# Two layers of linear attention and squared-ReLU MLP on one core: idle steps and new costs in the weave of layer 1, and the pair's weight sums in other buffers

## The chip, the cores and the metric

The kernel runs on one core of a Trainium2 chip. The core has five engines that run side by side and wait for each other through semaphores: TensorE (PE in the profile; its weight loads are PEld), VectorE (DVE), ScalarE (ACT), GpSimd (POOL) and SyncE (SP, which here only issues DMAs). The metric is the device time of one execution in microseconds; lower is better.

## The reference

x has 2048 rows of 576 numbers in float32. Four sublayers follow each other, A, B, A, B, with the same weights both times:

```python
def A(x):                     # linear attention, 32 heads of 18
    q, k, v = split_heads(x @ wqkv)
    phi = lambda t: concat(softmax(t @ w_phi), softmax(-(t @ w_phi)))
    kv, z = einsum("bhsf,bhsd->bhfd", phi(k), v), phi(k).sum(over rows)
    return (phi(q) @ kv / (phi(q) @ z + 1e-6)) @ wo
def B(x):                     # 576 -> 4608 -> 576
    h = x @ w1 + b1
    return relu(h)**2 @ w2 + b2
x = x + A(layernorm(x)); x = x + B(layernorm(x))      # layer 0
x = x + A(layernorm(x)); x = x + B(layernorm(x))      # layer 1
```

The sums kv and z run over all rows, so no row's attention output can be made before all rows' keys and values are in.

## The kernel before, in words

The rows are cut into four blocks of 512, a block into four tiles of 128. Nearly every product is made of three: operands are split into a high and a low part (`hi` by an ACT copy into the matmul's format, `lo` by a subtraction on DVE or POOL), and hi·hi, hi·lo and lo·hi are summed in PSUM. The names in the profile leave numbers out: `m_0` is the MLP of block 0, `a_2` the attention of block 2, `m_p` the pair (below).

The work around the change is in layer 1, whose blocks come in the order 1, 0, 3, 2.

**The weave.** `weave(main, other, rate)` (L99) runs two generators into one program. `main` is the MLP of a block (`g_mlp`), whose loop over 36 feature tiles f is cut into 36 steps; `other` is "the back", the attention work of later blocks. After each main step, `rate` is added to what is due, and steps of the back are issued while at least 1 is due; each takes off its cost, the number that it yields (1.0 where it yields nothing). `paced(gen, cost)` (L111) gives all steps of a generator one cost. `held` (L560) lets a step's instructions follow a given instruction of the MLP on its engine. The order of each engine is fixed when the program is built: the framework goes by the order in which instructions are written, and takes a later one first where it expects the earlier one still to wait. On the chip each engine then runs its queue strictly in that order, so an instruction that waits holds up what is queued behind it.

One main step, an MLP iteration: `first(f+1)` loads and splits weights (L697 to L709), `hidden(f)` makes 14 matmuls (L719), `square(f)` applies bias, ReLU and square on ACT (L726 to L728) and the low part on DVE (L729, the `hl` of the profile's `m_0hb`), and `second(f-1)` makes 15 matmuls of the second product (L746, L737). So the result of `square(f)` is wanted one iteration later. The last rows of a block are taken through buffers of tag "x" and written out (L785 to L793).

The back of the first weave of layer 1 (main: block 1, rate 3.6): features of block 0 (`g_features`: four softmax steps of cost 5.5, then per row tile two steps of cost 2.8 that divide by the denominators on DVE and POOL, L584 to L594), queries of block 3 (four steps, 1.0), output of block 0 (`g_out`: one step, ten of transposing and multiplying with kv, L624 and L640, and one, at 1.0 each), features of block 3, and then, for each row tile, the product with wo, the residual and the norm of block 0 (five steps, 3.0).

The back of the second weave (main: block 0, rate 4.3): output of block 3; its norm (`g_norm_first`: four steps with the product with wo at L673, then six that transpose, L818 and L826, and evict, L843 to L847; the result is spilled to memory, L850); queries of block 2 (four steps; they read spilled rows back, L374), features of block 2, output of block 2; its norm (`g_norm_second`, likewise four steps and then six). These six are four `main` tiles and, after the second and the fourth, a `tail`. In `g_norm_second` each is *combined*: from the two halves of the spilled block and of this one, `combine` (L893) makes the operands b22, t1, t2, t3, t4, and each is split; a main tile has six DVE operations there, five ACT copies (L917), two POOL sums (L905, L907) and four POOL low parts (L918). All ten steps of either norm cost 3.0. Then the prelude of the pair (seven steps, 2.0).

**PSUM.** In layer 1's weaves the back's transposes and products take tiles of tag "w", of which there are two; each must be evicted by ACT and DVE before it is used again.

**The pair.** The MLPs of blocks 3 and 2 are done together (`g_pair`), 18 times a pair of feature tiles: the first product of both blocks with two feature tiles is made by seven half-size products (L1007) in place of eight, which need sums of the weight quarters a11, a12, a21, a22. `load_pair` loads the quarters: a11 and a12 in one buffer, a21 and a22 in another, in turn of two pairs. `split_pair` makes the sums on POOL and splits the seven operands (hi L966 on ACT, lo L967 on DVE, a small band L969 on POOL):

```python
s1 = a21 + a22     # ss[0], L972
s2 = s1 - a11      # ss[1], L975
s4 = a12 - s2      # ss[3], L979
s3 = a11 - a21     # ss[2], L982
```

The four sums are in buffers of tag "x" (five buffers), which the rows of `g_mlp`'s end, of `g_out` and the temporaries of `combine` use too. The splits for pair k+1 are written between the products of pair k. In the products, u and v (tag "qk", five buffers) take the eviction of PSUM (L1117, L1118, L1121, L1122), and are written to memory (`hd`, L1125 and L1075) for the second block; `product(k, bx, "a22", ...)` can go on in bank bx only after L1122 has read it. The first pair's first products stand ahead of the last rows of the second weave's MLP.

Of the kernel before, what the change touches and what calls it, by code (L numbers as in the profile page):

```python
# [7 lines left out]
F32 = mybir.dt.float32  # L8
# [5 lines left out]
P = 128  # L14
# [7 lines left out]
def layers_kernel(  # L22
# [18 lines left out]
    nc = tc.nc  # L41
    S, D = x_in.shape[1], x_in.shape[2]
# [17 lines left out]
    HK = HP // P  # L60
# [8 lines left out]
    sb = ctx.enter_context(tc.tile_pool(name="sb", bufs=2))  # L69
# [39 lines left out]
        drain(other)  # L109

    def paced(gen, cost):  # L111
        for _ in gen:
            yield cost

    def lagged(n, produce, consume, by=1):

# [27 lines left out]
    for p, g in ((GW, slice(0, full)), (gw[full], slice(full, NG))):  # L144
        n = g.stop - g.start
# [165 lines left out]
    def moments(x, t, name):  # L311
        stats = sb.tile([P, 2, 6], F32, tag="bns", name=f"{name}s{t}")
        mv = sb.tile([P, 2], F32, tag="bnm", name=f"{name}m{t}")
        rstd = sb.tile([P, 1], F32, tag="rstd", name=f"{name}d{t}")
        for h in range(2):
            nc.vector.bn_stats(stats[:, h, :], x[:, h * HP : (h + 1) * HP])
        nc.vector.bn_aggr(mv, stats.rearrange("p a b -> p (a b)"))
        nc.gpsimd.tensor_scalar(rstd, mv[:, 1:2], EPS, None, op0=ALU.add)
        nc.gpsimd.tensor_tensor(rstd, rstd, mhalf, op=ALU.pow)
        return mv, rstd  # L320
# [472 lines left out]
            nc.sync.dma_start(out[b * TB + t * P : b * TB + (t + 1) * P] if layer else xs[b][t], x)  # L793


    def g_norm_halves(x_of, name, then, main, tail):

        xd = sb.tile([P, NT, 2 * TP], F32, tag="xd", name=f"{name}e", bufs=1)
        xns = []
        for t in range(NT):  # L800
            x = x_of(t)
            mv, rstd = moments(x, t, name)
            xn = sb.tile([P, D], F32, tag="qk", name=f"{name}n{t}", bufs=5)[:, : KC * P]
            x3 = x.rearrange("p (a d) -> p a d", a=2)
            nc.vector.tensor_scalar(xn.rearrange("p (a d) -> p a d", a=2), x3[:, :, : HK * P], mv[:, 0:1], rstd,
                                    op0=ALU.subtract, op1=ALU.mult)
            nc.vector.tensor_scalar(xd[:, t].rearrange("p (a r d) -> p a r d", a=2, r=3),
                                    x3[:, :, HK * P :].unsqueeze(2).to_broadcast([P, 2, 3, TW]),
                                    mv[:, 0:1], rstd, op0=ALU.subtract, op1=ALU.mult)
            then(t, x)  # L810
            xns.append(xn)
            yield
        for t in range(NT):
            pt = wtile(f"{name}p{t}")
            p4 = pt.rearrange("p (a c n) -> p a c n", a=2, n=P)
            for a in range(2):
                for c in range(HK):
                    nc.tensor.transpose(p4[:, a, c], xns[t][:, (a * HK + c) * P : (a * HK + c + 1) * P], ident)  # L818
            main(t, p4)
            yield  # L820
            if t % 2:
                pt = wtile(f"{name}p{NT}{t}")
                p3 = pt[:TP].rearrange("p (a n) -> p a n", a=2)
                for a in range(2):
                    for i in range(2):
                        nc.tensor.transpose(p3[:, a, i * P : (i + 1) * P],  # L826
                                            xd[:, t - 1 + i, a * TP : (a + 1) * TP], ident)
                tail(t // 2, p3)
                yield

    def g_norm_first(x_of, dst, name, then):

        tiles = {}

        def main(t, p4):
            if t == 0:
                tiles.update(xt_tiles(name))
                tiles["t"] = sb.tile([P, 2 * D], F32, tag="E", name=f"{name}t", bufs=4)[:TP, : 2 * TB]
                tiles["t"] = tiles["t"].rearrange("p (a n) -> p a n", a=2)
            rows = slice(t * P, (t + 1) * P)  # L840
            hi, lo = tiles["h"][:, :KC, rows], tiles["l"][:, :, rows]
            p3 = p4.rearrange("p a c n -> p (a c) n")
            nc.scalar.activation(hi, p3, AF.Copy)  # L843
            nc.vector.tensor_sub(lo, p3, hi.bitcast(F32))

        def tail(h, p3):
            nc.scalar.activation(tiles["t"][:, :, h * TB // 2 : (h + 1) * TB // 2], p3, AF.Copy)  # L847

        yield from g_norm_halves(x_of, name, then, main, tail)
        nc.sync.dma_start(pth, tiles["h"][:, :KC].rearrange("p c n -> p (c n)").bitcast(F32))  # L850
        nc.sync.dma_start(ptl, tiles["l"].rearrange("p c n -> p (c n)").bitcast(F32))
        nc.sync.dma_start(ptt, tiles["t"].rearrange("p a n -> p (a n)"))

    def g_norm_second(x_of, dst, name, then):
# [68 lines left out]
                split_tail(ops[k][2][:, cols], src)  # L923

        prepare()
        yield from g_norm_halves(x_of, name, then, main, tail)
        dst.update(ops)

    def g_pair(layer, blocks, x, after, name):
# [16 lines left out]

        def split_pair(k, raw):
            (a11, a12), (a21, a22) = raw
            ss = [sb.tile([P, D], F32, tag="x", name=f"{name}s{j}_{k}", bufs=5)[:, : (HK + 1) * P]
                  .rearrange("p (c n) -> p c n", c=HK + 1) for j in range(4)]  # L950
            width = NC * P
            if k % 2 == 0:
                one = sb.tile([P, NC * HP], F32R, tag="h1", name=f"{name}wa_{k}")
                two = sb.tile([P, NC, P], F32, tag="r1", name=f"{name}wb_{k}").rearrange("p c n -> p (c n)")
                homes = [new_slot(j, f"{name}wv{j}_{k}", F32R) for j in range(NT)] + [one[:, :width], one[:, width : 2 * width], two.bitcast(F32R)]
            else:
                t = xt_tiles(f"{name}wc_{k}")
                flat = [t[p].rearrange("p c n -> p (c n)") for p in "hl"]
                homes = [flat[0][:, j * width : (j + 1) * width] for j in range(4)]
                homes += [flat[1][:, j * width : (j + 1) * width] for j in range(3)]  # L960
            homes = dict(zip(("a11", "a12", "s1", "s2", "s4", "s3", "a22"), homes))

            def split(key, src):
                op = homes[key].rearrange("p (c n) -> p c n", c=NC)
                hi, lo = op[:, : HK + 1], op[:, HK + 1 :]
                nc.scalar.activation(hi, src, AF.Copy)  # L966
                nc.vector.tensor_sub(lo, src[:, :HK], hi[:, :HK].bitcast(F32))  # L967
                band = slice(2 * TW, 3 * TW)
                nc.gpsimd.tensor_sub(hi[band, HK], src[band, HK], hi[band, HK].bitcast(F32))  # L969
                wops[k, key] = (hi, lo)  # L970

            nc.gpsimd.tensor_add(ss[0], a21, a22)  # L972
            split("a11", a11)
            yield
            nc.gpsimd.tensor_sub(ss[1], ss[0], a11)  # L975
            split("a12", a12)
            yield
            split("s1", ss[0])
            nc.gpsimd.tensor_sub(ss[3], a12, ss[1])  # L979
            yield  # L980
            split("s2", ss[1])
            nc.gpsimd.tensor_sub(ss[2], a11, a21)  # L982
            yield
            split("s4", ss[3])
            yield
            split("s3", ss[2])
            yield
            split("a22", a22)
            yield
# [176 lines left out]
    def g_attend(layer, b, x, raws, dst, name, behind=None, norm=None, mid=(None, None), ph=None):  # L1166

        cost = (lambda c: c) if layer else (lambda c: None)
        if ph is None:
            ph = []  # L1170
            if raws is None:
                raws = []
                yield from g_queries(layer, b, x, raws, name)
            yield from g_features(layer, raws, ph, name)
        if mid[0]:
            yield from mid[0]
        yield from g_out(layer, b, ph, dst, name, behind=behind and behind["last"], norm=norm, mid=mid[1],
                         costs=(cost(1.0), cost(3.0)))

    def g_features(layer, raws, ph, name):  # L1180
        cost = (lambda c: c) if layer else (lambda c: None)
        er = []
        yield from paced(held(g_soft(raws, er, name)), cost(5.5))
        yield from paced(held(g_phi(layer, er, ph, name, True)), cost(2.8))
# [68 lines left out]
    x, xprev = xT[b], xT[prev]  # L1253
    for layer in range(2):
# [7 lines left out]
        for i, b in enumerate(order):  # L1262
            n = f"{layer}_{b}"
# [38 lines left out]
            back = g_back()  # L1302

            def then(back=back):
# [1 line left out]
                next(products)  # L1306

            weave(g_mlp(layer, b, ready, rows, f"m{n}", None if i else dense["turned"], then if layer and i == 1 else None),
                  back, (3.6, 4.3)[i] if layer else 1.5 if i else 1.0)
            ready, nxt_raws = nxt, None  # L1310
            if layer == 0:
                prev_rows = (b, rows)
        if layer == 0:
# [3 lines left out]
            x, xprev, vpair = {}, keep["x"], keep["v"]  # L1317
# [29 lines left out]
```

## Time and profile before

| | us |
|---|---|
| median of three runs | 2567.29 |
| lowest, highest run | 2564.45, 2567.36 |
| the profiled execution | 2566.98 |
| its span, first to last instruction | 2565.3 |

In the profile, L719 is line 719 of the kernel. A row of the timeline reads: start in us, duration in us, engine, line, operation, output and inputs, shapes, count, and in brackets the engine's idle time before it with what ended it. A row of a group reads: line, engine, operation, output and inputs, shapes, count, busy us in total, mean ns of one, idle us before and what ended it. A row of the stretches reads: from:to, length, then for PE, PEld, DVE, ACT and POOL the busy us and the number of instructions, the clock granted to TensorE (1.00 is full speed), and the DMA engines' busy share and GB/s.

### The profile page before, as it was taken

The numbers are of one execution on the slowest core, as the hardware profiler recorded it, in microseconds if no ns is written. First come the engines' busy times: TensorE is split into PE (matmuls) and PEld (weight loads), VectorE is DVE, ScalarE is ACT, GpSimd is POOL, SyncE is SP. The second block draws the span as 40 slices with busy tenths as digits, with TensorE's granted clock in tenths as the row PEclk, the third lists the DMA queues.
The fourth block names the chain that finished last, engine by engine and source line by source line (L and its number), as shares of the span: only waits on it lengthen the run. The fifth ranks groups of instructions, "written<-read, shape, count | busy, mean of one in ns | idle before, by whom it ended". The sixth has DMA issues, their size and how long they took to land. (4 is left out here: it accounts for less than half of the span.)

```text
span 2565.3 us, 41355 instructions
## 1 busy us (share of the span) xinstructions
PE 2508.4 (98%) x15282; PEld 2205.9 (86%) x15282; DVE 1540.2 (60%) x2408; ACT 1268.4 (49%) x2177; POOL 804.9 (31%) x869
## 2 busy tenths in 40 slices
PE   8998999999999999999999999999999999999999
PEld 8998888888888888888888988888888877888888
DVE  6778844456655467556434788484658565554444
ACT  4334554545554455545554445554455365666543
POOL 3544311113222132123111423132214256555222
PEclk9999999999999999999999999999999999999999
DMA  8102332354333533243433143233453333333364
GB/s 251 57 23 89 103 115 87 104 187 133 89 97 106 181 127 97 84 128 104 118 98 106 45 132 114 79 98 106 143 175 98 119 111 124 111 104 102 105 205 148
DMA packets 276758, 295.03 MB, mean 115 GB/s; under 512 B 28906, under 2 KB 206826, under 8 KB 274250
## 3 DMA queue, kind: packets, MB, share of 16 engines
q1 hardware_dynamic: 275296, 289.68, 36.7%
q8 instruction: 119, 1.95, 0.3%
q10 hardware_dynamic: 1258, 2.70, 0.3%
q14 instruction: 85, 0.70, 0.1%
HBM read 249.39 MB, written 42.89 MB: 114 GB/s over the span
## 5 line engine op out<-in xcount | busy, mean ns | idle before, releaser
L746 PE MATMUL m_0acc<-m_0s,m_0hb 128*128 128x448 f32 x864 | 200.2, 366 | 2.2 <-DVE m_0hb L729 2.2
L746 PE MATMUL m_1acc<-m_1s,m_1hb 128*128 128x448 f32 x864 | 199.2, 366 | 0.5 <-DVE m_1hb L729 0.5
L719 PE MATMUL m_0ph<-a_0nh,m_0h 128*128 128x512 f32 (+1 forms) x760 | 196.1, 386 | 3.4 <-ACT m_0hr L726 3.0
L746 PEld LDWEIGHTS m_0acc<-m_0s,m_0hb 128*128 128x128 f32 x864 | 161.6, 188 | 24.7 <-DVE m_0hb L729 3.9
L746 PEld LDWEIGHTS m_1acc<-m_1s,m_1hb 128*128 128x128 f32 x864 | 161.9, 188 | 21.4 <-DVE m_1hb L729 0.9
L719 PEld LDWEIGHTS m_0ph<-a_0nh,m_0h 128*128 128x128 f32 x760 | 136.4, 189 | 29.7 <-ACT m_0hr L726 3.7
L709 POOL TENSOR_TENSOR m_0s<-m_0r,m_0s 128x128 fp32r<-128x128 f32 x72 | 59.5, 826 | 316.0 <-ACT m_0s L705 279.9
L709 POOL TENSOR_TENSOR m_1s<-m_1r,m_1s 128x128 fp32r<-128x128 f32 x72 | 57.3, 795 | 306.4 <-ACT m_1s L705 274.4
L707 DVE TENSOR_TENSOR m_1h<-m_1r,m_1h 128x640 fp32r<-128x640 f32 x72 | 65.6, 912 | 121.6 <-ACT m_1h L704 121.5
L726 ACT ACTIVATE m_0hr<-m_0ph,b1t 128x512 f32<-128x512 f32 x72 | 49.3, 685 | 169.8 <-PE m_0ph L719 169.8
L707 DVE TENSOR_TENSOR m_0h<-m_0r,m_0h 128x640 fp32r<-128x640 f32 x72 | 65.9, 916 | 111.8 <-ACT m_0h L704 109.7
L726 ACT ACTIVATE m_1hr<-m_1ph,b1t 128x512 f32<-128x512 f32 x72 | 49.5, 688 | 152.7 <-PE m_1ph L719 152.7
L996 DVE TENSOR_TENSOR m_ps<-m_pr,m_ps 128x448 fp32r<-128x448 f32 x72 | 51.7, 718 | 97.5 <-ACT m_ps L995 96.6
L997 POOL TENSOR_TENSOR m_ps<-m_pr,m_ps 128x128 fp32r<-128x128 f32 x72 | 59.2, 822 | 133.9 <-ACT m_ps L995 127.9
L746 PE MATMUL m_2acc<-m_2s,m_2hb 128*128 128x448 f32 x432 | 99.7, 366 | 1.3 <-DVE m_2hb L729 1.3
L746 PE MATMUL m_3acc<-m_3s,m_3hb 128*128 128x448 f32 x432 | 99.5, 366 | 1.0 <-DVE m_3hb L729 1.0
L719 PE MATMUL m_1ph<-t1onh,m_1h 128*128 128x512 f32 (+1 forms) x380 | 97.5, 385 | 0.6 <-ACT t1onh L347 0.6
L719 PE MATMUL m_2ph<-a_2nh,m_2h 128*128 128x512 f32 (+1 forms) x380 | 97.2, 384 | 0.2 <-DVE m_2h L707 0.2
L719 PE MATMUL m_3ph<-t0onh,m_3h 128*128 128x512 f32 (+1 forms) x380 | 95.7, 382 | 0.1
L719 PE MATMUL m_1ph<-a_1nh,m_1h 128*128 128x512 f32 (+1 forms) x380 | 95.2, 381 | 0.0
L1036 PE MATMUL m_pacc<-m_ps,m_phb 128*128 128x448 f32 x432 | 93.9, 366 | 0.0
L995 ACT ACTIVATE m_ps<-m_pr 128x576 fp32r<-128x576 f32 x72 | 49.2, 684 | 87.9 <-PE m_pacacc L1026 65.7
(2103 smaller groups left out, 7131.5 us busy)
## 6 DMA issues: line engine op xcount, KB each, us to landing
m_0r<-in_B_w SPq DMA_DIRECT2D x72, 288.0 KB
m_1r<-in_B_w SPq DMA_DIRECT2D x72, 288.0 KB
m_pr<-in_B_w SPq DMA_DIRECT2D x72, 288.0 KB
m_0r<-in_B_w SPq DMA_DIRECT2D x72, 256.0 KB
m_1r<-in_B_w SPq DMA_DIRECT2D x72, 256.0 KB
m_3r<-in_B_w SPq DMA_DIRECT2D x36, 288.0 KB
m_2r<-in_B_w SPq DMA_DIRECT2D x36, 288.0 KB
m_3r<-in_B_w SPq DMA_DIRECT2D x36, 256.0 KB
```

Of the source, the lines that this page charges most:

```text
L707: nc.vector.tensor_sub(l1, r1, h1.bitcast(F32))
L709: nc.gpsimd.tensor_sub(s2[:, D + R : 2 * D], r2[:, R:], s2[:, R:D].bitcast(F32))
L719: nc.tensor.matmul(ph[:, cols], a, m, start=(k == 0), stop=(k == len(ops) - 1))
L726: nc.scalar.activation(hr, ph, AF.Relu, bias=b1t[:, f : f + 1])
L746: nc.tensor.matmul(acc[t][:, :R], a[:, rows], m, start=(f == 0 and k == 0), stop=(f == NF - 1 and k == 2))
L995: nc.scalar.activation(s2[:, :D], r2, AF.Copy)
L996: nc.vector.tensor_sub(s2[:, D : D + R], r2[:, :R], s2[:, :R].bitcast(F32))
L997: nc.gpsimd.tensor_sub(s2[:, D + R : 2 * D], r2[:, R:], s2[:, R:D].bitcast(F32))
L1036: nc.tensor.matmul(accs[b][t][:, :R], a[:, rows], m, start=(g == 0 and k == 0), stop=(g == NF - 1 and k == 2))
```

## The change

Three things are edited. The steps of the back of layer 1 get an idle step of cost 5.0 (a `yield` that issues nothing) ahead of each output, and the rates of its two weaves go from 3.6 and 4.3 to 3.7 and 5.0. In both norms by halves the four steps with the product with wo keep 3.0, while the six transposed tiles cost 1.0 in `g_norm_first` and 5.0 in `g_norm_second`; `paced` passes a generator's own cost on where its own is None. In `split_pair` s1 and s2 move to buffers of tag "qk", s3 is written over a21 and s4 over a12, and the order of the POOL operations changes. The number of compute instructions stays as it is.

```diff
     def paced(gen, cost):
-        for _ in gen:
-            yield cost
+        for own in gen:
+            yield own if cost is None else cost
...
-    def g_norm_halves(x_of, name, then, main, tail):
+    def g_norm_halves(x_of, name, then, main, tail, cost):
...
             then(t, x)
             xns.append(xn)
-            yield
+            yield 3.0
         for t in range(NT):
...
             main(t, p4)
-            yield
+            yield cost
             if t % 2:
...
                 tail(t // 2, p3)
-                yield
+                yield cost
...
     def g_norm_first(x_of, dst, name, then):
...
-        yield from g_norm_halves(x_of, name, then, main, tail)
+        yield from g_norm_halves(x_of, name, then, main, tail, 1.0)
...
     def g_norm_second(x_of, dst, name, then):
...
-        yield from g_norm_halves(x_of, name, then, main, tail)
+        yield from g_norm_halves(x_of, name, then, main, tail, 5.0)
...
         def split_pair(k, raw):
             (a11, a12), (a21, a22) = raw
-            ss = [sb.tile([P, D], F32, tag="x", name=f"{name}s{j}_{k}", bufs=5)[:, : (HK + 1) * P]
-                  .rearrange("p (c n) -> p c n", c=HK + 1) for j in range(4)]
+            ss = [sb.tile([P, D], F32, tag="qk", name=f"{name}s{j}_{k}", bufs=5)[:, : (HK + 1) * P]
+                  .rearrange("p (c n) -> p c n", c=HK + 1) for j in range(2)]
...
             nc.gpsimd.tensor_sub(ss[1], ss[0], a11)
             split("a12", a12)
             yield
+            nc.gpsimd.tensor_sub(a21, a11, a21)
             split("s1", ss[0])
-            nc.gpsimd.tensor_sub(ss[3], a12, ss[1])
-            yield
+            yield
+            nc.gpsimd.tensor_sub(a12, a12, ss[1])
             split("s2", ss[1])
-            nc.gpsimd.tensor_sub(ss[2], a11, a21)
-            yield
-            split("s4", ss[3])
-            yield
-            split("s3", ss[2])
+            yield
+            split("s4", a12)
+            yield
+            split("s3", a21)
             yield
             split("a22", a22)
             yield
...
     def g_attend(layer, b, x, raws, dst, name, behind=None, norm=None, mid=(None, None), ph=None):
...
             yield from g_features(layer, raws, ph, name)
+        if layer:
+            yield 5.0
         if mid[0]:
             yield from mid[0]
         yield from g_out(layer, b, ph, dst, name, behind=behind and behind["last"], norm=norm, mid=mid[1],
-                         costs=(cost(1.0), cost(3.0)))
+                         costs=(cost(1.0), cost(None if norm else 3.0)))
...
             weave(g_mlp(layer, b, ready, rows, f"m{n}", None if i else dense["turned"], then if layer and i == 1 else None),
-                  back, (3.6, 4.3)[i] if layer else 1.5 if i else 1.0)
+                  back, (3.7, 5.0)[i] if layer else 1.5 if i else 1.0)
```

## The prediction

> **What bounds the kernel now.** The page comes first: its head says how full each engine is.
>
> ```profile
> span 2565.3 us, 41355 instructions
> PE 2508.4 (98%) x15282; PEld 2205.9 (86%) x15282; DVE 1540.2 (60%) x2408; ACT 1268.4 (49%) x2177; POOL 804.9 (31%) x869
> ```
>
> PE works 2508.4 of 2565.3 us; the change alters no matmul, so it can win only PE's idle time, 56.9 us, and stretches in which PE is slow. It touches layer 1 alone, so the second view is the busy time by stretch from there on (length, then PE, PEld, DVE, ACT, POOL busy, granted clock, DMA):
>
> ```profile
> 1530.00:1800.00 270.00, 270.00 (x1354) 235.05 (x1353) 176.23 (x264) 139.54 (x223) 70.22 (x69) 0.99 0.35 103
> 1905.00:1975.00 70.00, 70.00 (x363) 61.99 (x362) 51.58 (x67) 38.49 (x61) 21.30 (x17) 1.00 0.28 82
> 1975.00:1993.00 18.00, 15.43 (x71) 12.25 (x70) 16.76 (x25) 7.51 (x12) 7.95 (x6) 1.00 0.46 134
> 1993.00:2066.00 73.00, 73.00 (x400) 63.81 (x399) 38.69 (x71) 31.44 (x55) 18.90 (x25) 1.00 0.35 110
> 2066.00:2097.00 31.00, 25.67 (x114) 20.86 (x113) 24.00 (x45) 20.49 (x47) 22.55 (x29) 0.94 0.29 85
> 2097.00:2127.00 30.00, 30.00 (x138) 25.11 (x137) 19.29 (x34) 17.37 (x33) 15.21 (x21) 1.00 0.49 150
> 2127.00:2138.00 11.00, 7.21 (x25) 5.32 (x24) 8.33 (x13) 6.31 (x12) 9.74 (x14) 0.84 0.33 98
> 2138.00:2440.00 302.00, 302.00 (x1346) 251.72 (x1346) 147.69 (x242) 187.38 (x344) 153.82 (x199) 1.00 0.35 111
> ```
>
> The first weave of layer 1 (1530 to 1800) and the pair's steady part (2138 to 2440) have no idle PE, so there is nothing to win there. Three holes are left, all in or just behind the second weave: 2.6 us at 1975, 5.3 at 2066, 3.8 at 2127. The waits of PE name them (waiter, awaited, us in total, times, longest):
>
> ```profile
> PE m_ppx L1007 <- DVE m_pu L1122: 3.4, 1, 3.4
> ...
> PE m_0ph L719 <- ACT m_0hr L726: 3.0, 2, 2.0
> ...
> PE a_2np L818 <- DVE a_2nl L918: 1.7, 1, 1.7
> ...
> PE a_2pn L640 <- DVE a_2fl L627: 1.2, 1, 1.2
> ...
> PE a_2qp L387 <- DMA a_2uh<-xth: 0.6, 1, 0.6
> ```
>
> In two of the holes the clock falls as well:
>
> ```profile
> 2072.88:2076.29 3.41, 3.13 (x7) 2.48 (x8) 2.90 (x6) 3.04 (x7) 0.64 (x2) 0.51 0.02 5
> 2134.41:2137.82 3.41, 3.12 (x8) 2.48 (x8) 2.48 (x5) 2.23 (x5) 2.70 (x4) 0.51 0.31 92
> ```
>
> Each has about 3.12 us of matmuls at half speed; at full speed they would take 1.56, so each costs 1.56 us beside its wait. The holes with their slow stretches come to 2.6 + 5.3 + 1.6 + 3.8 + 1.6 = 14.9 us, the DMA wait to 0.6. That is the most there is to win.
>
> **The change part by part.** Where each step lands is arithmetic on the code: every main step adds the rate, every step behind is issued while at least 1 is due and takes off its cost. I number the 36 main steps of a weave.
>
> *Combined tiles at 5.0, idle step, rate 5.0 (second weave).* Before, the second norm's transposed tiles come at steps 28 (main 0), 29 (main 1 and tail 0), 30 (main 2), 31 (main 3 and tail 1), the prelude at 32 to 35. Afterwards they have a step each, 24 to 29, and the prelude takes 30 to 32. The hole at 2066 begins behind the step with two. ACT shows why:
>
> ```profile
> 2070.17 0.42 ACT L917 ACTIVATE a_2nt4h<-a_2nu 128x256 fp32r<-128x256 f32 x1 [1.81 <-POOL a_2nu L907]
> ...
> 2072.44 0.67 ACT L726 ACTIVATE m_0hr<-m_0ph,b1t 128x512 f32<-128x512 f32 x1
> ```
>
> ACT stands 1.81 us for POOL's sum, the copies of main 1 and tail 0 follow, and the MLP's relu (L726) is queued behind them; PE waits for that relu, and for PSUM that the same tiles hold (L818). A main tile gives POOL this:
>
> ```profile
> L918 POOL TENSOR_TENSOR a_2nt1l<-a_2nu,a_2nt1h 128x256 fp32r<-128x256 f32 x1 | 0.7, 744 | 1.8 <-ACT a_2nt1h L917 1.8
> ...
> L918 POOL TENSOR_TENSOR a_2nt4l<-a_2nu,a_2nt4h 128x256 fp32r<-128x256 f32 x1 | 0.7, 737 | 0.0
> ```
>
> Six such operations (four of L918, L905, L907) by 0.74 are 4.4 us. The MLP's own POOL work is one operation an iteration, 0.83 us:
>
> ```profile
> L709 POOL TENSOR_TENSOR m_0s<-m_0r,m_0s 128x128 fp32r<-128x128 f32 x72 | 59.5, 826 | 316.0 <-ACT m_0s L705 279.9
> ```
>
> The 5.2 together fit into one MLP iteration, 6.35 us (five take 31.74, below). Main 0 already stands alone, at 2056, in the stretch 1993 to 2066 without idle PE. So I take the hole as closed: -5.3, and -1.6 for the clock.
>
> [...] The trace has the halving right behind the waits; I go by the trace.
>
> *Idle step ahead of the output, and rate 5.0 (hole at 1975).* The output's first transposes wait for the last feature tile from DVE and POOL. Here is what DVE has to do (five MLP iterations; then one feature tile with one iteration; then the MLP's own three operations in that stretch):
>
> ```profile
> 1928.95:1960.69 31.74, 31.74 (x146) 27.22 (x145) 25.74 (x37) 18.63 (x28) 10.34 (x10) 1.00 0.34 99
> 1964.39:1972.61 8.22, 8.22 (x40) 7.08 (x39) 8.08 (x12) 4.97 (x9) 4.47 (x4) 1.00 0.35 104
> ```
>
> ```profile
> L729 DVE TENSOR_TENSOR m_0hb<-m_0hr,m_0hb 128x512 fp32r<-128x512 f32 x6 | 7.5, 1250 | 0.0
> L707 DVE TENSOR_TENSOR m_0h<-m_0r,m_0h 128x640 fp32r<-128x640 f32 x6 | 7.1, 1188 | 0.0
> ...
> L708 DVE TENSOR_TENSOR m_0s<-m_0r,m_0s 128x448 fp32r<-128x448 f32 x5 | 4.6, 914 | 0.0
> ```
>
> A feature tile with an iteration is 8.2 us of DVE, of which the MLP has 1.25 + 1.19 + 0.91 = 3.35, so the tile has 4.9. Before, the four tiles start at step 17 and the output at 22: DVE needs 4 x 4.9 + 5 x 3.35 = 36.4 against 31.7, late by 4.6; the trace shows 2.6 of it. Afterwards they start at 13 and the output at 19: 4 x 4.9 + 6 x 3.35 = 39.7 against 38.1, late by 1.6. So the idle step wins about 1. But now a tile falls in each of four consecutive iterations, 8.2 against 6.35 each, a backlog of 7.4 by the last. The MLP's own hl (L729) stands in that queue, and PE asks for it one iteration (6.35) later, so about 1 us comes out at PE. I take 0 for the part: bounds -2.6 (output late no more) and +7.4 (no slack at all).
>
> *First norm's tiles at 1.0.* Before they are spread over steps 7 to 10; afterwards five come at step 7, the sixth with the queries at step 8. Only two PSUM buffers are free, and each must be emptied by
>
> ```profile
> L844 DVE TENSOR_TENSOR a_3nl<-a_3np,a_3nh 128x512 fp32r<-128x512 f32 x4 | 2.6, 679 | 0.0
> ...
> L843 ACT ACTIVATE a_3nh<-a_3np 128x512 fp32r<-128x512 f32 x4 | 2.1, 584 | 0.0
> ```
>
> 0.58 + 0.68 = 1.26 us. From the third tile on PE needs other work for that time; matmuls of the MLP are what covers it. Without any cover 3 x 1.26 = 3.8; with all, 0, as when two came together at 1872 (no idle PE in the wait list). I take 0.7. The queries come one step nearer to the spill that they read back; that load still starts when the last tail is copied, so its 0.6 stays. The output's steps come up to five a step, where four cost no idle at 1804 to 1840: 0.
>
> *First weave (3.7, idle step).* The output begins at step 15 instead of 14 and the norm ends at 34 instead of 33 of 36; PE has no hole there: 0. Last feature tiles are written one step later; the second weave's idle step makes room for them.
>
> *Sums in other buffers.* The chain of waits tells the hole at 2127 (start, us, what):
>
> ```profile
> 2120.74 2.34 DMA out<-m_0x
> ...
> 2123.30 1.03 POOL m_ps L975
> ...
> 2131.58 1.19 POOL m_ps L979
> ...
> 2132.79 0.53 ACT m_pwa L966
> ...
> 2133.35 0.63 DVE m_pwa L967
> 2133.98 0.67 DVE m_pu L1122
> ```
>
> The weight sums share the five "x" buffers with the MLP's four last tiles; POOL can write the sum only when the output has been written to memory (2.34 us). From 2123 POOL works the sums off one behind the other, DVE holds at the split of the last (L967), and the eviction that PE needs (L1122) is queued behind. In "qk" the sums need no output write and can run ahead of 2118. Then L1122 follows the previous DVE operation at once (and this is what PE does meanwhile):
>
> ```profile
> 2129.86 1.40 PE L746 MATMUL m_0acc<-m_0s,m_0hb 128*128 128x448 f32 x6
> ```
>
> ```profile
> 2129.94 0.74 DVE L1121 SCALAR_TENSOR_TENSOR m_pu<-m_ppy,b1t,m_pu 128x512 f32<-128x512 f32 x1
> ```
>
> L1121 ends at 2130.68, and L1122 with its 0.7 at 2131.4 instead of 2134.65. PE has matmuls until 2131.26, so 0.2 is left of 3.8: -3.6, and -1.6 for the clock. The edit adds one wait: the sum written over a12 must wait until ACT, DVE and POOL have split a12. It stands in POOL's queue, ahead of the small bands (L969) and the w2 low parts (L997); in steady state the splits are for a later pair, and PE is never idle there: 0.
>
> **Sum** against the profiled execution, 2566.98 us (1.7 above its span, 0.3 below the median 2567.29): -6.9 - 5.2 + 0.7 + 0 = -11.4, so 2555.6, or about 2556.
>
> **Rivals.** (a) *DVE becomes the bound in the features*: all of the 7.4 shows, with one slow stretch of 1.6. 2556 + 9 = 2565. For: DVE is busy 8.08 of 8.22 us already. Against: hl has nearly an iteration of slack. (b) *The pair's hole stays*, because the sum over a12 waits for its split and DVE again holds ahead of L1122: 5.2 back, 2561. Against: a12's split needs no sum. (c) *The order, not the spacing, makes ACT wait*: each lone main tile delays the relu, and the pair's hole moves on with it; nothing is won, 2567. Against: main 0. (d) *Slower: "qk" couples the sums to the hd writes.* u and v live in "qk" until written out; if the sums must wait for such a write in every pair, with PE behind them, the price is the 2.34 of a write 18 times, 42 us: 2598. It decides when a buffer comes round before its write has landed. Four of five buffers are taken per pair, so one comes round after 1.25 pairs, and a pair takes (2437.1 - 2155.9) / 16 = 17.6 us by
>
> ```profile
> L1075 SPq DMA_DIRECT2D hd<-m_pu x17: 320/345/382, 2155.9 to 2437.1; - x17
> ```
>
> That is 22 us against 2.3, so it would need sums that run over a pair ahead and hold their buffers.
>
> **How the numbers follow.** Forecast 55%, (a) 13%, (b) 13%, (c) 9%, (d) 10%. The forecast's own range is 2549 to 2561: all 14.9 + 0.6 won gives 2551.5, less 2.8 for the spread of the runs (2564.45 to 2567.36); the norm uncovered (+3.1) and part of the features give 2561. With (a) and (b) 81% is covered: 2549 to 2566. About 0.2%, 5.1 us, is what a measurement of this kernel can tell from no change. Faster by more: forecast and (b), 68%; within: (a) and (c), 22%; slower: (d), 10%.
>
> **What would show it.** Right: no wait of L719 for L726 and none of L818 in the second norm, clock 1.00 there; L975 not released by a write of out; L1122 straight behind L1121; the pair still 17.6 us. Wrong: waits for L729 or a longer wait of L624 at the features (a); L1122 behind L967 (b); POOL released by hd writes and PE idle after 2138 (d).

## The result, and the profile after

| | us |
|---|---|
| before, median of 20 runs (range) | 2566.82 (2564.45 to 2569.14) |
| after, median of 20 runs (range) | 2562.45 (2561.23 to 2566.13) |
| ratio of the two, 95% interval | 0.9985 [0.9978, 0.9992] |
| profiled execution, before and after | 2566.98 and 2562.01 |
| its span, before and after | 2565.3 and 2560.3 |

One run of the experiment e2 below took 3489.84 us at a granted clock of 0.654; the ratio given there leaves it out.

The change wins 4.4 us where 11.4 were forecast. The interval leaves 1 out, so it is faster, but by 0.15%, less than the 0.2% that was set as the bound of "no change". The head of the page shows the same number of operations on every engine, DVE 12.8 us busier than before, and a shorter span:

```profile
span 2560.3 us, 41339 instructions
...
PE 2508.3 (98%) x15282; PEld 2204.8 (86%) x15282; DVE 1553.0 (61%) x2408; ACT 1271.1 (50%) x2177; POOL 806.9 (32%) x869
```

Busy time by stretch, for the stages that the prediction went through (length; PE, PEld, DVE, ACT, POOL busy; granted clock; DMA share, GB/s):

```profile
1530.00:1800.00 270.00, 270.00 (x1352) 234.74 (x1351) 181.59 (x263) 139.38 (x223) 73.97 (x69) 0.99 0.36 102
1870.00:1878.00 8.00, 6.96 (x42) 5.77 (x41) 5.36 (x10) 5.16 (x10) 4.13 (x4) 1.00 0.71 221
...
1950.00:1966.00 16.00, 13.05 (x59) 10.55 (x59) 15.72 (x25) 6.30 (x10) 7.14 (x6) 1.00 0.34 102
...
2030.00:2070.00 40.00, 37.58 (x174) 31.53 (x174) 26.70 (x50) 22.86 (x49) 21.17 (x30) 0.96 0.30 86
...
2055.34:2058.75 3.41, 3.41 (x10) 2.64 (x9) 2.85 (x6) 1.87 (x5) 0.46 (x1) 0.51 0.29 86
2127.00:2134.00 7.00, 5.43 (x25) 4.32 (x24) 5.88 (x10) 4.39 (x8) 4.24 (x6) 1.00 0.41 135
...
2140.00:2440.00 300.00, 299.89 (x1337) 249.69 (x1336) 153.91 (x242) 190.99 (x345) 153.30 (x198) 1.00 0.34 105
```

The first weave (1530 to 1800) and the steady pair (2140 to 2440) are as full as before. Four places between them have idle PE, and one of these has a stretch at half clock (2055.34). The waits of PE from 1860 to 2160 name them (total us, times, longest):

```profile
PE m_0ph L719 <- ACT m_0hr L726: 3.2, 2, 2.3
PE m_0acc L746 <- DVE m_0hb L729: 2.9, 2, 1.5
PE m_ppx L1007 <- DVE m_pu L1122: 1.6, 1, 1.6
PE a_3np L826 <- DVE a_3nl L844: 1.0, 1, 1.0
```

Set against the wait list of before, place by place (a half-clock stretch counts 1.56 us, the prediction's estimate from 3.12 us of busy PE at 0.51):

| place | before | after | difference | forecast |
|---|---|---|---|---|
| first norm's tiles (L826 for L844) | 0 | 1.0 | +1.0 | +0.7 |
| query load (L387 for the spill) | 0.6 | 0 | -0.6 | 0 |
| features and output (L729, L624, L640) | 2.6 | 2.9 | +0.3 | 0 |
| second norm, waits | 5.3 | 3.2 | -2.1 | -5.3 |
| second norm, half clock | 1.6 | 1.6 | 0 | -1.6 |
| pair's start, waits | 3.8 | 1.6 | -2.2 | -3.6 |
| pair's start, half clock | 1.6 | 0 | -1.6 | -1.6 |
| sum | 15.5 | 10.3 | -5.2 | -11.4 |

The two profiled executions differ by 2566.98 - 2562.01 = 5.0, the medians by 4.4. So the table comes near the result, from one trace of each kernel, and 6.2 of the missing 7 us lie in two places: the second norm, where 4.8 of the forecast 6.9 didn't come, and the pair's start, 1.4.

**Second norm.** ACT's timeline about the longest wait (start, us, engine, line, operation; in brackets the idle time before it and what ended it):

```profile
2047.31 0.42 ACT L917 ACTIVATE a_2nt4h<-a_2nu 128x256 fp32r<-128x256 f32 x1 [1.32 <-POOL a_2nu L907]
2047.64 0.62 ACT L727 ACTIVATE m_0hb<-m_0hr 128x512 fp32r<-128x512 f32 x1
...
2051.51 0.42 ACT L890 ACTIVATE a_2nt1t<-a_2nu 96x256 fp32r<-96x256 f32 x1 [1.53 <-DVE a_2nu L899]
...
2052.77 0.42 ACT L890 ACTIVATE a_2nt4t<-a_2nu 96x256 fp32r<-96x256 f32 x1 [0.38 <-POOL a_2nu L905]
...
2054.14 0.67 ACT L726 ACTIVATE m_0hr<-m_0ph,b1t 128x512 f32<-128x512 f32 x1
```

Main tile 1 makes ACT stand 1.32 us for POOL's sum (L907), with the MLP's own copies (L727, then L704) queued behind. DVE's L707 waits for L704, and tail 0, one iteration later, begins on DVE only behind the MLP's L707, L729 and L708:

```profile
2048.91 0.83 DVE L707 TENSOR_TENSOR m_0h<-m_0r,m_0h 128x640 fp32r<-128x640 f32 x1 [2.77 <-ACT m_0h L704]
...
2050.25 0.89 DVE L708 TENSOR_TENSOR m_0s<-m_0r,m_0s 128x448 fp32r<-128x448 f32 x1
2051.07 0.41 DVE L899 TENSOR_TENSOR a_2nu<-a_2np,a_2nf 96x256 f32<-96x256 f32 x1
```

So the relu (L726) comes 2.33 us after PE asks for it. A tile alone doesn't do that: main 0, one iteration ahead of main 1, made ACT stand as long (1.33 us), and PE waited behind neither of the two. The third tile in three neighbouring iterations does it, when the lateness has added up. The other wait, 0.9 us, comes with main 3, the fifth.

**Pair's start.** POOL still works the sums off just then, and DVE holds at a split ahead of the eviction that PE needs:

```profile
2127.87 1.08 POOL L981 TENSOR_TENSOR m_pr<-m_pr,m_ps 128x384 f32<-128x384 f32 x1
```

```profile
2128.98 0.52 ACT L966 ACTIVATE m_pwa<-m_pr 128x384 fp32r<-128x384 f32 x1 [1.50 <-POOL m_pr L981]
```

```profile
2128.00 0.74 DVE L1121 SCALAR_TENSOR_TENSOR m_pu<-m_ppy,b1t,m_pu 128x512 f32<-128x512 f32 x1
2128.66 0.57 DVE L967 TENSOR_TENSOR m_pwv<-m_ps,m_pwv 128x256 fp32r<-128x256 f32 x1
2129.54 1.30 DVE L967 TENSOR_TENSOR m_pwa<-m_pr,m_pwa 128x256 fp32r<-128x256 f32 x2 [0.31 <-ACT m_pwa L966]
2130.77 0.74 DVE L1122 SCALAR_TENSOR_TENSOR m_pu<-m_ppx,b1t,m_pu 128x512 f32<-128x512 f32 x1
```

No write of `out` releases POOL any more, as forecast; but L1122 doesn't follow L1121: three splits stand between, 2.1 us.

### The profile page after: what moved, and what is told of

Read it like the earlier page. It is cut to its first block, busy times and chain, and to the rows that moved or that the text cites. A ratio compares the mean times of both kernels' runs of the same rounds, so it can differ in the third digit from the quotient of the medians.

```text
span 2560.3 us, 41339 instructions
## 1 busy us (share of the span) xinstructions
PE 2508.3 (98%) x15282; PEld 2204.8 (86%) x15282; DVE 1553.0 (61%) x2408; ACT 1271.1 (50%) x2177; POOL 806.9 (32%) x869
## 5 line engine op out<-in xcount | busy, mean ns | idle before, releaser
L707 DVE TENSOR_TENSOR m_1h<-m_1r,m_1h 128x640 fp32r<-128x640 f32 x72 | 66.1, 920 | 116.0 <-ACT m_1h L704 116.0
L707 DVE TENSOR_TENSOR m_0h<-m_0r,m_0h 128x640 fp32r<-128x640 f32 x72 | 65.7, 913 | 115.8 <-ACT m_0h L704 112.7
L726 ACT ACTIVATE m_0hr<-m_0ph,b1t 128x512 f32<-128x512 f32 x72 | 49.3, 685 | 158.6 <-PE m_0ph L719 158.6
L726 ACT ACTIVATE m_1hr<-m_1ph,b1t 128x512 f32<-128x512 f32 x72 | 49.5, 687 | 153.2 <-PE m_1ph L719 153.2
L997 POOL TENSOR_TENSOR m_ps<-m_pr,m_ps 128x128 fp32r<-128x128 f32 x72 | 63.5, 882 | 184.2 <-ACT m_ps L995 160.7
L996 DVE TENSOR_TENSOR m_ps<-m_pr,m_ps 128x448 fp32r<-128x448 f32 x72 | 45.1, 627 | 102.3 <-ACT m_ps L995 102.3
L746 PEld LDWEIGHTS m_2acc<-m_2s,m_2hb 128*128 128x128 f32 x432 | 80.8, 188 | 12.4 <-DVE m_2hb L729 2.2
```

Of the source, the lines that this page charges most:

```text
L707: nc.vector.tensor_sub(l1, r1, h1.bitcast(F32))
L726: nc.scalar.activation(hr, ph, AF.Relu, bias=b1t[:, f : f + 1])
L746: nc.tensor.matmul(acc[t][:, :R], a[:, rows], m, start=(f == 0 and k == 0), stop=(f == NF - 1 and k == 2))
L996: nc.vector.tensor_sub(s2[:, D : D + R], r2[:, :R], s2[:, :R].bitcast(F32))
L997: nc.gpsimd.tensor_sub(s2[:, D + R : 2 * D], r2[:, R:], s2[:, R:D].bitcast(F32))
```

## The experiments

Three theories came out of the traces. *Relay and queue in the norm*: POOL's sum for t4, between DVE and ACT, delays what is queued behind it on ACT; rivals are the order of the tiles and their sheer number. *Queue in the pair*: the splits stand ahead of L1122. *Full DVE in the features*: one tile in every iteration makes hl late. All medians beside their ratio to before, with the 95% interval:

| kernel | median us | ratio to before |
|---|---|---|
| before with the new buffers alone (e1) | 2566.40 | 0.9994 [0.9986, 1.0003] |
| after with the old buffers (e2) | 2563.11 | 0.9985 [0.9976, 0.9994] |
| after, features slower (e4) | 2559.37 | 0.9967 [0.9955, 0.9980] |
| after, combined tiles at 7.5 (e5) | 2557.54 | 0.9960 [0.9947, 0.9974] |
| after, t4 sums on DVE (e6) | 2556.76 | 0.9960 [0.9947, 0.9972] |
| after, splits behind the eviction (e7) | 2559.26 | 0.9967 [0.9955, 0.9980] |
| after, no idle steps (e9) | 2563.00 | 0.9981 [0.9972, 0.9990] |
| e4, e5 and e7 together (e10) | 2551.54 | 0.9939 [0.9927, 0.9952] |
| e10, t4 sums on DVE, tiles at 5.0 (e11) | 2552.02 | 0.9943 [0.9931, 0.9956] |
| e10 with the old buffers (e12) | 2559.09 | 0.9971 [0.9960, 0.9983] |
| before, t4 sums on DVE (e13) | 2560.97 | 0.9977 [0.9968, 0.9986] |
| e13 with the new buffers (e14) | 2557.42 | 0.9966 [0.9954, 0.9979] |

### The two halves of the change (e1, e2)

e1 is the kernel before with the `split_pair` of the diff; e2 is the changed kernel with the `split_pair` of before.

> The kernel before with the buffer part of the change alone (sums in qk and over a12, a21); paces and idle steps as before. Theory A (the parts are independent): only the pair's hole shrinks, from 3.8 us of wait and one half-speed stretch to about 1.6 us of wait without it, so about 2567 - 3.8 = 2563; the waits at the features (2.6 us) and at the second norm (5.3 us and its slow stretch) stay. Rival B (the earlier prelude of the new pace is what frees the pair): the hole stays as before, 2567, and L975 still starts near the last output write.

> The changed kernel with the sums of the kernel before (four buffers of tag x), so paces and idle steps alone. Theory A: the pair's hole is that of before, 3.8 us and a slow stretch, and the rest is that of after: second norm 3.2 us and one slow stretch, features 3.0 us, first norm 1.0 us; about 2567 - 1.5 = 2565.5. Rival B: the pair's hole is gone or below 2 us, about 2562.5.

The weave alone gives nearly all that the change gives, the buffers alone hardly anything in the median. e2's time is rival B's, but its pair still waits, 2.0 us for L1122 and 0.5 for L1118, with a stretch at half clock (2133.0 to 2136.4, 0.50): less than theory A's 3.8, more than rival B's 2. No sum of POOL waits for a write of `out` there, though the buffers are the old ones, so the earlier prelude alone ends that wait; L1122 is queued behind three splits on DVE, as in the changed kernel.

e1's runs fall into two groups, 2563.7 to 2564.6 (five, at a mean granted clock of 0.993 to 0.995) and 2566.4 to 2570.6 (six, five of them at 0.989 to 0.992, one at 0.994). Its profile, of a run of 2564.6, shows that the buffers did act. The waits of PE, and the stretches at half clock:

```profile
PE a_2np L818 <- DVE a_2nl L918: 3.2, 1, 3.2
PE m_0ph L719 <- ACT m_0hr L726: 2.7, 2, 2.1
PE m_ppx L1007 <- DVE m_pu L1122: 1.6, 1, 1.6
```

```profile
2071.50:2078.30 6.80, 6.20 (x16) 4.74 (x17) 6.18 (x12) 4.08 (x9) 2.01 (x3) 0.50 0.19 55
...
2091.90:2095.30 3.40, 3.40 (x10) 2.63 (x9) 2.96 (x7) 3.19 (x7) 2.00 (x3) 0.51 0.46 127
```

The pair's wait fell from 3.4 to 1.6, and no half clock is left there (granted clock 1.00 from 2124 to 2134). The second norm, which stands ahead of it in time, took this back in this run: 5.9 us of waits in place of 5.3, and half clock for 10.2 us in place of 3.4. The six slower runs have no trace. At the pair the profile agrees with theory A, the median agrees with B. So e1 alone couldn't say what the buffers are worth; e13 and e14 below do.

### The second norm (e5, e6)

```diff
-        yield from g_norm_halves(x_of, name, then, main, tail, 5.0)
+        yield from g_norm_halves(x_of, name, then, main, tail, 7.5)    # e5
...
-            nc.gpsimd.tensor_sub(t4, c21[0], t2)
+            nc.vector.tensor_sub(t4, c21[0], t2)                       # e6
...
-                nc.gpsimd.tensor_add(t4, t4, c21[1])
+                nc.vector.tensor_add(t4, t4, c21[1])
```

> The changed kernel with the combined tiles at 7.5 instead of 5.0, so a tile every one and a half iterations. Theory Order (the relu L726 stands behind a tile's copies in ACT's fixed queue, and these wait for POOL; the room between tiles does not matter): waits of L719 for L726 stay at about 3 us with their slow stretch, 2562.5. Rival Volume (a tile's work does not fit one iteration beside the MLP's): with half an iteration more the waits go to 0, 2562.5 - 3.2 - 1.6 = 2557.7.

> The changed kernel with the two sums for t4 (L905, L907) on DVE instead of POOL. Theory Relay (a tile is slow because its last operand goes DVE, POOL, POOL, ACT, where ACT stands 1.3 us for POOL with the relu queued behind): without the two POOL steps the relu comes over 1 us earlier in each tile, the waits of L719 for L726 fall from 3.2 to below 1 us and the slow stretch goes, about 2562.5 - 2.5 - 1.6 = 2558.5. Rival Start (the tile starts late, because its first DVE operation is queued behind L708, and nothing in its later steps matters): waits of about 3 us, 2562.5.

Both close the hole. In e5 (first fence) and e6 (second) PE waits for the relu 0.5 us in all, with no half clock (the mean granted clock of the profiled run is 0.995 in both, 0.993 in the changed kernel):

```profile
PE m_0ph L719 <- ACT m_0hr L726: 0.5, 1, 0.5
```

```profile
PE m_0ph L719 <- ACT m_0hr L726: 0.5, 2, 0.3
```

In e6 the tiles stand at 5.0 as in the changed kernel; only the two POOL sums are gone from between DVE and ACT. Tail 0's copies then run to the relu almost without a stop:

```profile
2048.20 0.42 ACT L890 ACTIVATE a_2nt4t<-a_2nu 96x256 fp32r<-96x256 f32 x1 [0.24 <-DVE a_2nu L905]
...
2049.18 0.67 ACT L726 ACTIVATE m_0hr<-m_0ph,b1t 128x512 f32<-128x512 f32 x1
```

So Volume, the rival of e5, holds, and the order of the tiles isn't at fault: e6 keeps it and has no hole. Start, the rival of e6, fails. The relay is at fault as long as a tile comes in every iteration: in e5 tiles come in two iterations out of three, and the free one lets the MLP catch up, as well as a shorter chain does (e6). The two runs don't tell whether moving POOL's work or shortening the chain counts more, since e6 does both.

### The features (e4, e9)

```diff
-        yield from paced(held(g_soft(raws, er, name)), cost(5.5))
-        yield from paced(held(g_phi(layer, er, ph, name, True)), cost(2.8))
+        yield from paced(held(g_soft(raws, er, name)), cost(6.4 if raws is slow[0] else 5.5))       # e4
+        yield from paced(held(g_phi(layer, er, ph, name, True)), cost(3.26 if raws is slow[0] else 2.8))
...
-        if layer:                                                                                   # e9
-            yield 5.0
```

`slow[0]` marks the queries of block 2, so e4 gives its features the pace of before (6.4 / 5.0 = 5.5 / 4.3).

> The changed kernel with the features of block 2 at costs 6.4 and 3.26 instead of 5.5 and 2.8, which at rate 5.0 is the pace of before (0.8 tiles an iteration), idle step kept. Theory (DVE has 8.2 us for a tile and an iteration in which PE takes 6.35, so one tile an iteration makes the low part of the square late): the two waits of L746 for L729 (1.4 and 1.6 us) go, the output's transposes still wait for nothing because of the idle step, about 2562.5 - 3 = 2559.5. Rival (the waits come from how tile and MLP operations are ordered on DVE, whatever the pace): waits of the same sum, 2562.5; or they move to L624, 2.6 us, 2562.

> The changed kernel without its idle steps (all three), rates and costs as changed. Theory Full DVE (the last feature tile is done near 1964.6, and with one iteration less the output's transposes come at about that time): they wait 0 to 1 us; the waits of L746 for L729 stay at 3 us; the second norm is as in the changed kernel; 2562.5 within 1. Rival Idle step needed (the hole of before at the features, 2.6 us, opens again beside the 3 us): 2565.

In e4 hl is late by 0.2 in place of 2.9 (first fence), and the output still doesn't wait. In e9 hl is as late as in the changed kernel, and the output waits again (second fence):

```profile
PE m_0acc L746 <- DVE m_0hb L729: 0.2, 1, 0.2
```

```profile
PE m_0acc L746 <- DVE m_0hb L729: 3.0, 2, 1.6
...
PE a_2pn L640 <- DVE a_2fl L627: 0.9, 1, 0.9
```

So the idle step does what it says, 0.9 us of wait and 0.5 in the median (the intervals of e9 and of the changed kernel overlap), and the features at one tile an iteration cost more at hl (2.9, against 0.3 before) than the idle step wins at the output.

### The pair's start (e7)

```diff
-                nc.vector.tensor_sub(lo, src[:, :HK], hi[:, :HK].bitcast(F32))
+                with tc.issue_after(freed[k - 2].ins) if k > 1 else nullcontext(): nc.vector.tensor_sub(lo, src[:, :HK], hi[:, :HK].bitcast(F32))
...
-                nc.vector.scalar_tensor_tensor(v, bx, bias(f1), v, op0=ALU.add, op1=ALU.add)
+                freed[k] = nc.vector.scalar_tensor_tensor(v, bx, bias(f1), v, op0=ALU.add, op1=ALU.add)
```

The first line is L967, the second L1122: the splits of pair k are put behind the eviction of pair k - 2 on DVE.

> The changed kernel with the low parts (L967) of pair k held behind the eviction L1122 of pair k-2 on DVE. Theory Queue (the 1.6 us that are left at the pair's start are DVE standing at the splits of pair 2, whose sums POOL has not finished, with L1122 queued behind): L1122 follows L1121, the wait falls to 0.3 us or less, about 2562.5 - 1.4 = 2561; the pair's steady part is unchanged. Rival Late splits (held back, the splits of pair 2 are late for their products): a new wait of L1007 for L966, L967 or L969 between 2150 and 2180, 2562.5 or more.

L1122 now waits for PE alone, not PE for it, and the pair has no idle PE left. DVE's timeline:

```profile
2126.09 0.74 DVE L1121 SCALAR_TENSOR_TENSOR m_pu<-m_ppy,b1t,m_pu 128x512 f32<-128x512 f32 x1
2127.53 0.75 DVE L1122 SCALAR_TENSOR_TENSOR m_pu<-m_ppx,b1t,m_pu 128x512 f32<-128x512 f32 x1 [0.69 <-PE m_ppx L1007]
```

The 1.6 us left at the pair were the queue's, as theory Queue had it, and rival Late splits is out. The median fell by 3.2, though, where 1.4 were expected. In e7's profile the half-clock stretch of the second norm is missing too (granted clock 1.00 from 2030 to 2080), though the edit is to the pair alone (last section, on the clock).

### All of it, and what the buffers are worth (e10 to e14)

e10 joins e4, e5 and e7, with the idle step kept only where features were made just before. e11 is e10 with the sums of e6, the combined tiles at 5.0 and the first norm's at 3.0; e12 is e10 with `split_pair` of before (and the hold of e7); e13 is the kernel before with the sums of e6; e14 is e13 with the new `split_pair`.

> All that has helped or should help: features of block 2 at 6.4 and 3.26, combined tiles at 7.5, evictions first in the pair, and no idle step ahead of the first output of the second weave. Theory (the waits are independent): the changed kernel less 3.1 for the features, 4.9 for the tiles and 1.4 for the pair, 2553. Rival (the slack is shared: what one part wins another loses, because the prelude now ends only at step 35): above 2556, with waits at the pair's start of over 2 us.

> The version with slow features, spaced tiles and the held split (2551.5 us), but with the two sums of t4 (L905, L907) on DVE in place of POOL, the combined tiles back at cost 5.0, and the first norm's tiles at 3.0 in place of 1.0. Theory Relay (what makes the relu late in the second norm is POOL's sum between DVE and ACT, not the spacing): with the sums on DVE, 5.0 is wide enough; PE's waits for the relu stay under 0.5 us, the 0.95 us of the first norm's tiles is gone, 2550 us. Rival Spacing (only a cost of 7.5 gives the relu room): waits of 1.5 us or more for L726 come back, 2552.5 us.

> The version with slow features, spaced tiles and the held split (2551.5 us), but with the pair's weight sums in four buffers of tag x as in the kernel before, and in its order on POOL; the hold of L967 behind L1122 is kept. Theory Buffers matter: POOL's sums of pair 1 wait for the writes of the last rows again, the splits behind them are late and PE waits 2 to 4 us at the pair's start, 2554.5 us. Rival Hold alone (what made PE wait was only the split ahead of L1122 in DVE's queue): no wait at the pair's start, 2551.5 us.

> The kernel before with one thing changed: the two sums of t4 (L905, L907) on DVE in place of POOL. Theory Relay: the second norm's waits of 5.3 us fall to 1 us or less and the half-speed stretch behind them goes, 1.6 us; the pair's hole stays at 3.8 us with its own stretch: 5.9 us less than before, 2561 us. Rival Crowd (two tiles in one iteration are too much for ACT, wherever the sums are made): 3 us or more of waits stay there, 2565 us.

> The kernel before with the t4 sums on DVE and the pair's sums in the new buffers: the buffer edit, without the second norm's hole ahead of it. Theory Independent (the buffers win 2 to 4 us at the pair, which the norm's varying hole hid when they were changed alone): 3 us less than the version with the DVE sums alone, near 2558 us. Rival Absorbed (something behind, such as the pair's first products, gives back what the buffers win): within 1 us of that version.

e10 wins 10.9 us on the changed kernel; e4, e5 and e7 alone win 3.1, 4.9 and 3.2, 11.2 together. So the three parts add up, and rival Shared slack is out. That the holes are independent isn't shown by it: the profile of each of the three lacks the half-clock stretch of the second norm, 1.6 us, which only e5 set out to remove (the granted clock is 1.00 from 2030 to 2080 in e4 and e7), and in e4 and e7 the relu waits are longer than in the changed kernel (4.4 and 4.6 against 3.2). e10 and e11 have the lowest medians here, and can't be told apart. What PE still waits for in e10 from 1800 to 2160:

```profile
PE m_0ph L719 <- ACT m_0hr L726: 1.0, 1, 1.0
PE a_3np L826 <- DVE a_3nl L844: 0.9, 1, 0.9
```

e11 misses its 2550 by 2. The wait of the first norm is gone, but the relu waits are longer than theory Relay had them, and the time is e10's:

```profile
PE m_0ph L719 <- ACT m_0hr L726: 1.5, 3, 0.9
```

Rival Spacing had named just this, 1.5 us or more and 2552.5. In this pace the relay isn't all that makes the relu late at 5.0.

e12 is slower than e10 by 7.5 us, more than either side expected, and the hold doesn't stand in for the buffers. POOL waits for the rows' write again, and new waits of PE, for L1108, come in the pair, the longest with a stretch at half clock behind it (e12's timeline of POOL, the waits of its whole trace, the stretch):

```profile
2114.04 1.01 POOL L975 TENSOR_TENSOR m_ps<-m_ps,m_pr 128x384 f32<-128x384 f32 x1 [0.82 <-DMA out<-m_0x]
```

```profile
PE m_ppx L1007 <- DVE m_pz L1108: 3.4, 3, 2.1
```

```profile
2134.60:2138.00 3.40, 3.40 (x10) 2.62 (x10) 0.67 (x2) 2.73 (x6) 0.39 (x2) 0.55 0.46 127
```

With an estimated 1.6 for the stretch, 0.5 for L1122 and 0.3 for L782 these are 5.8 of the 7.5; PE's waits don't show the rest.

e13 shows what the relay costs in the kernel before: 2560.97 against 2567.12 in the same series, 6.1 less, where 5.9 were expected. The hole isn't wholly closed. Its second norm waits 1.0 for L918 and 1.6 (the longest of two) for hl in place of 5.3, between theory Relay's 1 and rival Crowd's 3, without half clock (granted clock 1.00 from 2060 to 2095); and the pair's 3.5 stays, with half clock behind it (granted clock 0.50 in the 3.41 us from 2128.74):

```profile
PE m_ppx L1007 <- DVE m_pu L1122: 3.5, 1, 3.5
PE m_0acc L746 <- DVE m_0hb L729: 1.9, 2, 1.6
...
PE a_2np L826 <- DVE a_2nl L918: 1.0, 1, 1.0
```

e14 is 3.5 below e13, and its pair waits 1.6, without half clock (granted clock 1.00 from 2123 to 2130): the buffers are worth 3.5 us here, theory Independent. What they are worth depends on what stands beside them: 7.5 between e12 and e10, 0.5 in e1, and 0.7 between the medians of e2 and the changed kernel. And e14, which leaves the weave as it was and changes two lines beside the buffers, is 5.0 us faster than the changed kernel.

## Why the prediction was wrong

**The step that failed**, with 4.8 of the 7 us, is the one on the combined tiles: "The 5.2 together fit into one MLP iteration, 6.35 us", "Main 0 already stands alone", "So I take the hole as closed". It compared POOL's *work* with the length of an iteration. What holds PE is a *latency* in two queues that run in order: DVE to POOL to ACT for t4, 1.3 us of ACT standing, with the MLP's L727 behind it, and the next relu (L726) late in turn. POOL had time enough; ACT stood nevertheless. And main 0 was no evidence, since it is the first tile: nothing is late before it, and what it makes late shows only with the tiles behind it. Of the forecast 5.3 of waits and 1.6 of clock 2.1 came. e6, which takes the relay away, and with it some of POOL's work, closes the hole; e5 shows that room between the tiles does it too. In e11 and e13, where the relay is away as well, 1.5 and 2.6 us of waits are left, so it isn't the whole of the cause in every pace.

**Pair's start**: the mechanism was right (the sums no longer wait for the write; e14, 3.5 us) and the size 1.4 off. The forecast put all of it down to the buffers; e2 shows that the earlier prelude ends the wait for the write as well. "L1122 then follows the previous DVE operation at once" failed; rival (b) had the split ahead of L1122, and its time, 2561, is nearest to the one measured. It named the split over a12 (L981), which is what ACT waited 1.50 us for. Its reason, a sum that waits for a12's own split, doesn't show: POOL goes from L969 to L981 without a stop. And it priced the hole as staying whole, and it stayed by less than half. e7 shows the queue as the cause of what stayed.

**Features**: 0 was forecast as a balance of an output wait that shrinks and an hl wait that grows, and +0.3 came; both halves were larger than forecast. The output's 2.3 went wholly and 2.9 stand at hl (rival (a)'s 9 us didn't come). e4, which has neither, shows that this balance was no necessity: 3.1 us were to be had at the old pace with the idle step.

**First norm**: +0.7 forecast, 1.0 measured. **Query load**: its 0.6 was said to stay and went; it is gone in e1 too, which leaves the weave as it was. **First weave, steady pair, rival (d)**: no idle PE from 1530 to 1800, 0.1 us from 2140 to 2440, as forecast. One operation of POOL waits for an `hd` write there, 3.0 us; it is the low part L997, not a sum, and PE stays full. **Rival (c)**, nothing won because order makes ACT wait, had the right engine and the wrong price; and e5, which alters the spacing alone, closes the hole, against its "not the spacing".

The clock term was taken as one stretch for each hole. One of two went; the second norm's stayed, behind a wait of 2.33 us, while e7 had none there behind one of 2.4 (below).

What stays open: why most of e1's slower runs have a lower clock; where the last 1.7 of the 7.5 us go in e12; how much of e4's and e7's win is the missing half-clock stretch; and the 0.8 us between the table's 5.2 and the median's 4.4, which is within the spread of the runs.

## What to carry to other kernels

When work is paced into gaps of a bound engine, don't compare its busy time with the gap: write down, for each helper engine, what stands in its queue ahead of the instruction that the bound engine wants, and what that waits for. Here a relay over three engines had ACT stand for 1.32 us, with the MLP's copies queued behind it and DVE's L707 waiting for one of them, and the lateness was carried into the next iteration, so a first item without a wait proved nothing for those behind it. A stall that is removed may be refilled by a varying one behind or ahead of it; to size one edit, first cure the neighbouring hole (e13, e14) and then make the edit.

## What the runs showed of the hardware

**The clock.** The stretches at half clock are 3.41 us long (from 2055.34 in the changed kernel, at 0.51), or twice that (6.80 in e1, from 2071.50, at 0.50). I estimate from the granted clock, 0.51, that each 3.41 us cost half of PE's busy time in it: 1.56 us each in the kernel before, 1.7 in the changed kernel, where PE worked through all of it. The length of the wait ahead alone doesn't decide: at the same place of the second norm the changed kernel had half clock behind 2.33 us, while e7, with a wait of 2.4 there, had none in the whole norm:

```profile
PE m_0ph L719 <- ACT m_0hr L726: 4.6, 3, 2.4
```

In the traces of the kernel before and of the changed kernel all changes of the clock are whole multiples of 3.413 us apart (17 and 13 distances, the longest 1249.28 us, 366 of them). In the changed kernel the wait falls into the 3.41 us just ahead of the half clock, and PE is busy for 1.08 of them (first fence); in e7 it is divided between two such stretches, with 2.26 and 2.19, and the clock stays at 1.00 (second fence):

```profile
2051.89:2055.30 3.41, 1.08 (x7) 0.75 (x6) 3.00 (x8) 2.62 (x7) 0.72 (x1) 1.00 0.44 116
```

```profile
2048.97:2052.39 3.42, 2.26 (x13) 1.78 (x11) 3.29 (x8) 1.35 (x4) 1.15 (x2) 1.00 0.64 180
2052.39:2055.80 3.41, 2.19 (x9) 1.80 (x10) 2.57 (x6) 3.38 (x7) 0.00 (x0) 1.00 0.01 2
```

In the kernel before PE was busy for 0.95 and 0.35 us of the 3.41 us ahead of its two stretches. So a wait of over 2 us had an estimated 1.7 us more of cost behind it in one run and nothing in another.

**DVE beside POOL.** In the features of the changed kernel two-input operations of DVE took 1.66 and 1.99 us (timeline of DVE), each ending about 0.6 us behind the POOL operation that had begun before it (timeline of POOL: 1944.97 + 1.69 = 1946.66 against 1945.55 + 1.66 = 1947.21; 1948.51 against 1949.13):

```profile
1945.55 1.66 DVE L729 TENSOR_TENSOR m_0hb<-m_0hr,m_0hb 128x512 fp32r<-128x512 f32 x1
1947.14 1.99 DVE L594 TENSOR_TENSOR a_2Q1e<-a_2Q1e,a_2Q1r 128x576 f32<-128x576 f32 x1
```

```profile
1944.97 1.69 POOL L594 TENSOR_TENSOR a_2Q1e<-a_2Q1e,a_2Q1r 128x576 f32<-128x576 f32 x1 [3.22 <-DVE a_2Q1r L589]
1946.63 1.88 POOL L584 TENSOR_TENSOR a_2m<-a_2Q2e,zb 128x576 f32<-128x576 f32 x1
```

In e4 the same DVE operation began 0.11 us ahead of POOL's, and took 0.76:

```profile
1967.12 0.76 DVE L594 TENSOR_TENSOR a_2Q3e<-a_2Q3e,a_2Q3r 128x576 f32<-128x576 f32 x1
```

```profile
1967.23 1.68 POOL L594 TENSOR_TENSOR a_2Q3e<-a_2Q3e,a_2Q3r 128x576 f32<-128x576 f32 x1 [5.09 <-DVE a_2Q3r L589]
```

So of the DVE operations in these rows the two that began behind POOL's took 1.66 and 1.99 us, and the one that began ahead of POOL's 0.76. POOL's own L594 took the same in both orders (1.69 and 1.68). It is one part of why hl is late in a crowded iteration: L729 takes 1.66 us here, and 0.68 where no POOL operation was under way when it began (at 2041.64).
